# Pooled attention and two feed-forwards: the second one's products in blocks of 384 tokens over two batches, with another table of ranks

## The chip, the cores and the metric

The kernel runs on one core of a Trainium2 chip. Its metric is device time in microseconds, as the median over runs; lower is better. Beside the timed runs there is one execution that the hardware profiler recorded; all rows below are from that one.

## The reference, cut to what matters

The three stages run one after the other on 4 batches, 8 heads, 1152 keys and 576 pooled queries of 64 values, so on 2304 tokens of 512 values. The inputs are float32.

```python
q_pool = q.reshape(B, H, S // 2, 2, D).mean(axis=3)
p = exp(scores - max);  attn = p / (sum(p) + 1e-9);  x = attn @ v       # scores = q_pool k^T / 8
x = (s * relu(x @ w_in) ** 2 + b) @ w_out                               # d_ff 2048
out = (sigmoid(x @ w_gate) * (x @ w_val)) @ w_out2                      # d_ff 1536
```

## The kernel before, in words

All matrix products run on TensorE (PE) in a 32-bit format with fewer bits than float32, so each operand is split into a high part and a low part (`hi`, `lo`), and a product is three matmuls: high by high, high by low, low by high (`mm3`, lines 529 to 535; the three matmuls are lines 531, 532 and 533 for both feed-forwards). The split of a tile is a cast for the high part (line 455 on ScalarE, line 457 on GpSimd) and a subtraction for the low part (line 465, on VectorE or GpSimd). ScalarE is ACT in the rows, VectorE is DVE, GpSimd is POOL.

A batch is 576 tokens (`SQ`), half of one is 288 (`HQ`). The attention of batch 0 is laid out by rows (`pair_rows`), the others by columns (`pair_half`): scores (line 760), a running maximum, its transposition (773) and spreading (738), subtraction (468), exponential (786), split, and the products with the values (808, 809 for the high part, 813 for the low part). The first feed-forward (`ffn1`) runs once per batch, and its matmuls stand between those of the attention of the next batch. The second (`ffn2`) runs twice, each time over two batches: the first call for batches 0 and 1, then the first feed-forward of batch 3, then the second call for batches 2 and 3.

In `ffn2` a feature tile is 128 of the 1536 hidden features. For each one the weights of gate and value are fetched, decoded on three engines (lines 489 to 499) and split into one of four slots called `w` (`ROOM`, w=4), and the gate and value products are made with `up`: per batch and half, 12 matmuls of 288 columns into a PSUM bank for the gate and 12 for the value. Sigmoid (line 1023, ACT), product (line 468, DVE) and a split into `h` follow. After each four feature tiles come the products with `w_out2` (lines 1038 to 1040, 512 columns), 12 for each of nine tiles of 128 tokens. Three `raw` slots hold weights that are being decoded.

The order of all instructions on all engines is planned in Python before the program is written. `Plan.order` walks through time with assumed durations; whenever an engine is free it takes, of the operations whose inputs and slots are at hand, the one with the lowest rank. A rank is a number for the kind of work plus an amount from the table `MOVED` (lines 38 to 151), and ties go by the place in the program plus a second amount from that table. So a change of that table, or of what the operations are, can move any instruction. Each engine then works through its own list in order; what it waits for on the chip are semaphores of the single tiles.

Of the kernel before, what the change touches and what calls it, by code (L numbers as in the profile page):

```python
# [11 lines left out]
F32 = mybir.dt.float32  # L12
F32R = mybir.dt.float32r
AF = mybir.ActivationFunctionType
ALU = mybir.AluOpType
# [23 lines left out]
    "q load": (8, -97),  # L39
    "k load": (16, 21),  # L40
    "v load": (58, -139),
    "v hi": (-33.5, 17),
    "v lo": (-5, -53),
    "q add": (56.5, -16),
    "q twice": (60, -3),
    "pr qT": (0, -105),
    "pr q hi False": (1.5, -26),
    "pr q lo False": (10, 70),
    "pr q hi True": (40, 70),
    "pr q lo True": (4, -76),  # L50
    "pr kT": (-7, 0),
    "pr k hi": (-23.5, 64),
    "pr k lo": (4.5, 94),
    "s b load": (51, 101),
    "r qk 1": (0, 436),
    "r max": (20, 94),
    "r - max": (-33.5, 116),
    "r exp": (59.5, -13),
    "r pT": (-31, -29),
    "r p": (-29.5, -47),  # L60
    "r p hi": (-7.5, -76),
    "r p lo": (-26.5, 53),
    "r pv": (-40, 67),
    "r pT hi": (-20, 30),
    "r pT lo": (32.5, 157),
    "r o": (-40, 104),
    "r x add": (27, -30),
    "r qk 2": (-29, -108),
    "r sums": (1.5, -33),
    "r sums eps": (-0.5, -100),  # L70
    "r 1 / sums": (30, -110),
    "r spread": (-40, -92),
    "r rows": (-3, 63),
    "r rows mid": (0, 533),
    "r x / sums": (0.5, 3),
    "r x / sums mid": (52, 49),
    "r end": (-1, -100),
    "ps qT": (-6.5, -120),
    "ps q hi False": (60, 55),
    "ps q lo False": (-21, 2),  # L80
    "ps kT": (-16, 90),
    "ps k hi": (2, 116),
    "ps k lo": (-33.5, 42),
    "xx hi": (8, 64),
    "xx lo": (0, -25),
    "w load": (-40, -77),
    "w top": (-14.5, 44),
    "w scale": (-24.5, -15),
    "w low": (-21, -21),
    "w join": (0, 65),  # L90
    "w sign": (-30, -67),
    "w hi": (-33, -111),
    "w lo": (-40, 113),
    "w keep": (-34.5, 128),
    "ff xx up": (42.5, -17),
    "ff relu": (0, -85),
    "square": (0.5, 119),
    "g hi": (0.5, 88),
    "g lo": (-2, 74),
    "ff down": (31, 10),  # L100
    "column sums": (60, -1),
    "column sum": (37.5, 56),
    "ff y": (-28.5, 61),
    "ff y add": (19, 52),
    "bias": (0, -21),
    "y bias": (0, -25),
    "y store": (0, -54),
    "qk": (3.5, -109),
    "s copy": (4, -73),
    "s max": (7.5, 39),  # L110
    "max T": (0.5, 25),
    "max": (60, 105),
    "max rows": (26.5, 9),
    "s - max": (22, -81),
    "exp": (0, 89),
    "p hi": (-29.5, 0),
    "p lo": (54.5, -68),
    "pv hi": (22, 11),
    "pv lo": (31, 60),
    "sums": (26, -2),  # L120
    "x": (38, -115),
    "sums out": (-35, 44),
    "sums in": (-9.5, 84),
    "1 / sums spread": (0, -60),
    "1 / sums out": (-12, -13),
    "1 / sums in": (22.5, -70),
    "x / sums": (17, 25),
    "1 / sums": (24.5, -96),
    "w fetch": (-8, 31),
    "w come": (0, -52),  # L130
    "x store": (-3, -88),
    "turn": (-9, -110),
    "yy load": (16.5, -72),
# [4 lines left out]
    "gate val": (-25.5, 123),
    "h hi": (0, -7),
    "h lo": (59.5, 88),  # L140
    "down 2": (-7, 35),
    "out": (-23, -57),
    "out add": (11, -115),
    "out store": (0, -50),
    "xx load": (-40, 35),
    "p2 xx up": (-1.5, 75),
    "p2 relu": (0, -42),
    "p2 down": (0, 97),
    "p2 y": (0, -29),
    "p2 y add": (8, 19),  # L150
# [986 lines left out]
```

## Time and profile before

| what | us |
|---|---|
| median of three runs | 1469.33 (1465.91 to 1474.76) |
| the profiled execution's own time | 1465.83 |
| its span, first to last instruction | 1464.1 |
| PE busy in the span | 1402.4 (96%) |
| DVE, ACT, POOL busy | 1075.5, 944.4, 777.3 |

Matmuls are pipelined: one lasts some 295 ns in the record while the next starts 133 ns after it. So how long a row of matmuls takes is read from the distance of their starts, and "busy" is the time in which at least one runs.

### The profile page before, as it was taken

The numbers are of one execution on the slowest core, as the hardware profiler recorded it, in microseconds if no ns is written. First come the engines' busy times: TensorE is split into PE (matmuls) and PEld (weight loads), VectorE is DVE, ScalarE is ACT, GpSimd is POOL, SyncE is SP. The second block draws the span as 40 slices with busy tenths as digits, with TensorE's granted clock in tenths as the row PEclk, the third lists the DMA queues.
The fourth block names the chain that finished last, engine by engine and source line by source line (L and its number), as shares of the span: only waits on it lengthen the run. The fifth ranks groups of instructions, "written<-read, shape, count | busy, mean of one in ns | idle before, by whom it ended". The sixth has DMA issues, their size and how long they took to land. (4 is left out here: it accounts for less than half of the span.)

```text
span 1464.1 us, 26453 instructions
## 1 busy us (share of the span) xinstructions
PE 1402.4 (96%) x9868; PEld 1334.4 (91%) x9868; DVE 1075.5 (73%) x1775; ACT 944.4 (65%) x2017; POOL 777.3 (53%) x641
## 2 busy tenths in 40 slices
PE   7988999999889999999999999999999999999998
PEld 6877889988889999999899999989898999989897
DVE  6889898799888888889889656848583127847562
ACT  6899888888788989898989734434141534433130
POOL 3677566778766666656747535726151004726130
PEclk9999999999999999999999999999999999999999
DMA  3335132455442324142432374513144444323122
GB/s 90 93 113 194 38 103 91 147 170 164 141 138 103 114 81 137 32 152 72 138 111 75 109 270 148 176 53 122 36 138 126 154 160 144 109 71 109 36 67 65
DMA packets 103049, 167.97 MB, mean 115 GB/s; under 512 B 44652, under 2 KB 80264, under 8 KB 93832
## 3 DMA queue, kind: packets, MB, share of 16 engines
q1 hardware_dynamic: 96008, 115.95, 25.6%
q0 software_dynamic: 6912, 50.33, 9.8%
q8 instruction: 77, 1.26, 0.4%
q14 instruction: 52, 0.43, 0.1%
HBM read 139.99 MB, written 26.28 MB: 114 GB/s over the span
## 5 line engine op out<-in xcount | busy, mean ns | idle before, releaser
L465 POOL TENSOR_TENSOR pp<-st,pp 128x864 fp32r<-128x864 f32 x106 | 226.5, 2144 | 47.5 <-ACT pp L455 41.2
L532 PE MATMUL banks<-yy,w 128*128 128x288 f32 x768 | 226.3, 295 | 0.4 <-DVE yy L465 0.4
L533 PE MATMUL banks<-yy,w 128*128 128x288 f32 x768 | 226.4, 295 | 0.0
L531 PE MATMUL banks<-yy,w 128*128 128x288 f32 x768 | 226.0, 294 | 0.0
L462 ACT COPY st<-banks 128x288 f32<-128x288 f32 x432 | 153.7, 409 | 43.3 <-PE banks L760 35.6
L468 DVE TENSOR_TENSOR mx<-banks,mx 128x288 f32<-128x288 f32 x336 | 151.5, 451 | 22.8 <-ACT st L462 12.9
L760 PE MATMUL banks<-qT,kT 128*128 128x288 f32 x864 | 163.0, 302 | 5.2 <-DVE mx L468 2.6
L531 PE MATMUL banks<-xx,w 128*128 128x288 f32 x512 | 155.6, 304 | 4.6 <-DVE mx L468 2.4
L533 PE MATMUL banks<-xx,w 128*128 128x288 f32 x512 | 151.6, 296 | 0.0
L532 PE MATMUL banks<-xx,w 128*128 128x288 f32 x512 | 151.5, 296 | 0.0
L468 DVE TENSOR_TENSOR st<-st,banks 128x864 f32<-128x864 f32 x144 | 149.3, 1043 | 2.7 <-PE banks L738 2.6
L532 PEld LDWEIGHTS banks<-yy,w 128*128 128x128 f32 x768 | 144.0, 188 | 1.0 <-DVE yy L465 0.6
L531 PEld LDWEIGHTS banks<-yy,w 128*128 128x128 f32 x768 | 144.1, 188 | 0.4
L533 PEld LDWEIGHTS banks<-yy,w 128*128 128x128 f32 x768 | 144.0, 188 | 0.0
L786 ACT ACTIVATE st<-st 128x864 f32<-128x864 f32 x144 | 132.9, 933 | 12.9 <-DVE st L468 12.0
L489 POOL TENSOR_SCALAR raw<-raw 128x512 f32<-128x512 f32 x102 | 84.2, 826 | 106.1 <-DMA raw<-in_moe_w_gate_dram 43.3
L760 PEld LDWEIGHTS banks<-qT,kT 128*128 128x128 f32 x864 | 127.7, 188 | 11.1 <-DVE mx L468 5.6
L531 PE MATMUL banks<-g,w 128*128 128x288 f32 x448 | 135.5, 302 | 0.9 <-DVE mx L468 0.8
L533 PE MATMUL banks<-g,w 128*128 128x288 f32 x448 | 132.0, 295 | 0.0
L532 PE MATMUL banks<-g,w 128*128 128x288 f32 x448 | 132.0, 295 | 0.0
L808 PE MATMUL banks<-pp,vt 128*128 128x288 f32 x432 | 123.6, 306 | 5.3 <-ACT pp L455 2.4
L492 ACT ACTIVATE raw<-raw 128x512 f32<-128x512 f32 x104 | 71.6, 688 | 75.7 <-POOL raw L489 73.6
(150 smaller groups left out, 3968.2 us busy)
## 6 DMA issues: line engine op xcount, KB each, us to landing
w<-d_1u_1u POOLq DMA_DIRECT2D x24, 1024.0 KB, 5.9
w<-d_1d_1d POOLq DMA_DIRECT2D x24, 1024.0 KB, 5.7
raw<-in_moe_w_out_dram SPq DMA_DIRECT2D x40, 512.0 KB, 3.6
raw<-in_moe_w_gate_dram SPq DMA_DIRECT2D x24, 512.0 KB, 4.8
raw<-in_moe_w_val_dram SPq DMA_DIRECT2D x24, 512.0 KB
qn<-in_q_dram SPq DMA_DIRECT2D x16, 576.0 KB, 4.0
kn<-in_k_dram SPq DMA_DIRECT2D x32, 288.0 KB, 4.6
vn<-in_v_dram SPq DMA_DIRECT2D x32, 288.0 KB, 3.2
```

What stands on the lines that cost most here:

```text
L462: act(name, n, lambda: nc.scalar.copy(out=out(), in_=in_()), r, w, rank, sbuf=False)
L465: shared(name, n, lambda e: ENGINE[e].tensor_tensor(out=out(), in0=in0(), in1=in1(), op=op), r, w, rank, 2.15)
L468: dve(name, n, lambda: nc.vector.tensor_tensor(out=out(), in0=in0(), in1=in1(), op=op), r, w, rank)
L489: shared("w top", 512, lambda e: ENGINE[e].tensor_scalar(out=words(1).bitcast(F32), in0=words(1).bitcast(F32), scalar1=F64_TOP, scalar2=-F ...
L492: act("w scale", 512, lambda: nc.scalar.mul(words(1).bitcast(F32), words(1).bitcast(F32), 2.0 ** -112), [], [top], rank)
L531: nc.tensor.matmul(ps(), lhsT=whi(), rhs=xhi(), start=first, stop=False)
L532: nc.tensor.matmul(ps(), lhsT=whi(), rhs=xlo(), start=False, stop=False)
L533: nc.tensor.matmul(ps(), lhsT=wlo(), rhs=xhi(), start=False, stop=last)
L760: nc.tensor.matmul(ps.t[:, :HQ], lhsT=kT.t[:, c], rhs=qq[:, w, hf * HQ:(hf + 1) * HQ], start=(w == 0), stop=(w == 1))
L786: act("exp", 3 * HQ, lambda s=s: nc.scalar.activation(out=s.t, in_=s.t, func=AF.Exp), [], parts, AT)
L808: nc.tensor.matmul(acc.t[:, :HQ], lhsT=vt.t[:, 3 * i + c, D:], rhs=hi.t[:, c], start=(i == c == 0), stop=False)
```

## The change

The gate and value products are made in blocks of `TB` = 384 tokens over the two batches of a call, three blocks in place of four halves of 288. For that the input of a call lies in one tile over both batches (`yy`, one slot of 1152 columns in place of two of 576), `up` takes a slice of tokens instead of a half, and sigmoid, product and split work on 384 columns. The split's parts are now kept apart by block, and a tile of 128 tokens in the second product lies in one block, where before the middle one lay in two batches. Every entry of the table `MOVED` has other numbers.

```diff
-    yy=2, yl=1, h=4, fo=9,
+    yy=1, yl=1, h=4, fo=9,
...
-    "p2 yy up": (57.5, 61),
-    "gate": (-40, 69),
+    "p2 yy up": (51, -50),
+    "gate": (22, 37),
...
+    TB = 384
...
-    def up(tag, xx, w, hf, to):
+    def up(tag, xx, w, cs, to):
         ph = bank(tag)
-        cs = slice(hf * HQ, (hf + 1) * HQ)
+        n = cs.stop - cs.start
+        bs = range(cs.start // SQ, (cs.stop - 1) // SQ + 1)
         for kk in range(KC):
...
-                f"{tag} {xx.tag} up", lambda: ph.t[:, :HQ], HQ,
+                f"{tag} {xx.tag} up", lambda: ph.t[:, :n], n,
...
-                [ph, (w, 0), (w, 1), (xx, 0, kk), (xx, 1, kk)], kk == 0, kk == KC - 1, [to],
+                [ph, (w, 0), (w, 1), *((xx, i, kk, b) for i in range(2) for b in bs)], kk == 0, kk == KC - 1, [to],
...
     def ffn2(b0, nb, gate, here=None):
-        yy = [load_split("fy", "yy", y_d[b0 + b], [("y_d", b0 + b)], gate, here if b == nb - 1 else None) for b in range(nb)]
+        yy = slot("fy", "yy", [P, 2, KC, nb * SQ], F32R)
+        for b in range(nb):
+            load_split("fy", "yy", y_d[b0 + b], [("y_d", b0 + b)], gate, here if b == nb - 1 else None, yy, b)
...
-                for b in range(nb):
+                for i in range(nb * SQ // TB):
                     r = slot("fr", "r", [P, SQ])
-                    bs = slice(b * SQ, (b + 1) * SQ)
-                    for hf in range(2):
-                        cs = slice(hf * HQ, (hf + 1) * HQ)
-                        pg = up("p2", yy[b], wg, hf, r)
-                        pv = up("p2", yy[b], wv, hf, r)
-                        act("gate", HQ, lambda r=r, cs=cs, pg=pg: nc.scalar.activation(
-                            out=r.t[:, cs], in_=pg.t[:, :HQ], func=AF.Sigmoid), [pg], [(r, hf)], FE, sbuf=False)
-                        tt_dve("gate val", HQ, lambda r=r, cs=cs: r.t[:, cs], lambda pv=pv: pv.t[:, :HQ],
-                               lambda r=r, cs=cs: r.t[:, cs], ALU.mult, [pv], [(r, hf)], FE)
-                    split_g(gg, lambda gg=gg, bs=bs: gg.t[:, 0, bs], lambda gg=gg, bs=bs: gg.t[:, 1, bs], r,
-                            (gg, 0, b), (gg, 1, b))
+                    cs = slice(i * TB, (i + 1) * TB)
+                    pg = up("p2", yy, wg, cs, r)
+                    pv = up("p2", yy, wv, cs, r)
+                    act("gate", TB, lambda r=r, pg=pg: nc.scalar.activation(
+                        out=r.t[:, :TB], in_=pg.t[:, :TB], func=AF.Sigmoid), [pg], [r], FE, sbuf=False)
+                    tt_dve("gate val", TB, lambda r=r: r.t[:, :TB], lambda pv=pv: pv.t[:, :TB],
+                           lambda r=r: r.t[:, :TB], ALU.mult, [pv], [r], FE)
+                    split_g(gg, lambda gg=gg, cs=cs: gg.t[:, 0, cs], lambda gg=gg, cs=cs: gg.t[:, 1, cs],
+                            lambda r=r: r.t[:, :TB], TB, [r], (gg, 0, i), (gg, 1, i))
...
-                bs = sorted({m * P // SQ, ((m + 1) * P - 1) // SQ})
+                block = m * P // TB
```

The planned order differs on every engine; two places are shown. Line numbers of the changed kernel are one higher up to `up` and two higher behind it. In the names, `g`, `h` and `xx` are split inputs, a number behind a name is the tile's.

**The first call of `ffn2`.** PE before: the last products of batch 2's first feed-forward (tiles `g_927`, `g_929` with the weights `w_931`) and what follows them.

```order
L532 MATMUL banks_105<-g_927_10824,w_931_10753 128x288
L533 MATMUL banks_105<-g_927_10824,w_931_10753 128x288
L531 MATMUL banks_105<-g_929_10886,w_931_10753 128x288
L532 MATMUL banks_105<-g_929_10886,w_931_10753 128x288
L533 MATMUL banks_105<-g_929_10886,w_931_10753 128x288
L531 MATMUL banks_105<-yy_1149_10502,w_1161_10778 128x288
L532 MATMUL banks_105<-yy_1149_10502,w_1161_10778 128x288
L533 MATMUL banks_105<-yy_1149_10502,w_1161_10778 128x288
L531 MATMUL banks_105<-yy_1151_10629,w_1161_10778 128x288
L532 MATMUL banks_105<-yy_1151_10629,w_1161_10778 128x288
```

They all stand ahead of the second gate product of the call (`yy_1149` and `yy_1151` are the two batches, `w_1161` the first gate and value weights). PE in the changed kernel: the same kind of products (weights `w_930`), behind the first four feature tiles and the nine token tiles of the call, at the point where the fifth feature tile's weights `w_1194` are first used.

```order
L532 MATMUL banks_105<-g_929_10984,w_931_10748 128x288
L533 MATMUL banks_105<-g_929_10984,w_931_10748 128x288
L534 MATMUL banks_105<-g_929_10984,w_931_10748 128x288
L532 MATMUL banks_105<-g_922_10757,w_930_10735 128x288
L533 MATMUL banks_105<-g_922_10757,w_930_10735 128x288
L534 MATMUL banks_105<-g_922_10757,w_930_10735 128x288
L532 MATMUL banks_105<-g_924_10800,w_930_10735 128x288
L533 MATMUL banks_105<-g_924_10800,w_930_10735 128x288
L534 MATMUL banks_105<-g_924_10800,w_930_10735 128x288
L532 MATMUL banks_105<-yy_1148_10505,w_1194_11472 128x384
L533 MATMUL banks_105<-yy_1148_10505,w_1194_11472 128x384
```

So in the changed kernel the two slots `w_930` and `w_931` are held through most of the first call, and the call's own weights pass through the other two. POOL in the changed kernel, around the two instructions that write the value half of `w_1194`, whose slot was that of `w_1188`:

```order
L466 TENSOR_TENSOR h_1184_11233<-r_1186_11225,h_1184_11233 128x384
L458 TENSOR_SCALAR w_1191_11299<-raw_1193_11210 128x512
L466 TENSOR_TENSOR w_1191_11299<-raw_1193_11210,w_1191_11299 128x512
L490 TENSOR_SCALAR raw_1196_11316<-raw_1196_11316 128x512
L490 TENSOR_SCALAR raw_1202_11331<-raw_1202_11331 128x512
L458 TENSOR_SCALAR w_1194_11472<-raw_1196_11316 128x512
L466 TENSOR_TENSOR w_1194_11472<-raw_1196_11316,w_1194_11472 128x512
L490 TENSOR_SCALAR raw_1203_11490<-raw_1203_11490 128x512
L490 TENSOR_SCALAR raw_1209_11506<-raw_1209_11506 128x512
```

Before, this engine writes parts of the tile `w_1191` of the same feature tile; its slot was that of `w_1173`, whose last matmul stands a whole group of products earlier.

```order
L465 TENSOR_TENSOR w_1191_11413<-raw_1192_11281,w_1191_11413 128x512
L465 TENSOR_TENSOR w_1191_11413<-raw_1193_11331,w_1191_11413 128x512
L457 TENSOR_SCALAR h_1182_11477<-r_1183_11391 128x576
L465 TENSOR_TENSOR h_1182_11477<-r_1183_11391,h_1182_11477 128x576
L489 TENSOR_SCALAR raw_1199_11451<-raw_1199_11451 128x512
L489 TENSOR_SCALAR raw_1204_11467<-raw_1204_11467 128x512
L457 TENSOR_SCALAR w_1197_11591<-raw_1199_11451 128x512
L465 TENSOR_TENSOR w_1197_11591<-raw_1199_11451,w_1197_11591 128x512
```

**One softmax of the attention of batch 1.** PE before, at the spreading of its maximum (`mc_493`) and then, 24 matmuls of `xx_275` after it, up to its first product with the values (`pp_494`):

```order
L809 MATMUL banks_105<-pp_485_4054,vt0_121 64x288
L738 MATMUL banks_105<-ident_60,mc_493_4083 128x96 x3
L531 MATMUL banks_105<-xx_275_905,w_324_3578 128x288
L532 MATMUL banks_105<-xx_275_905,w_324_3578 128x288
L533 MATMUL banks_105<-xx_275_905,w_324_3578 128x288
L531 MATMUL banks_105<-xx_275_905,w_324_3578 128x288
```

```order
L760 MATMUL banks_105<-qT_447_3635,kT_449_3586 128x288 x6
L813 MATMUL banks_105<-pp_486_4126,vt0_121 128x288 x3
L808 MATMUL banks_105<-pp_487_4130,vt0_121 128x288
L809 MATMUL banks_105<-pp_487_4130,vt0_121 64x288
L808 MATMUL banks_105<-pp_487_4130,vt0_121 128x288
L809 MATMUL banks_105<-pp_487_4130,vt0_121 64x288
L808 MATMUL banks_105<-pp_487_4130,vt0_121 128x288
L809 MATMUL banks_105<-pp_487_4130,vt0_121 64x288
L760 MATMUL banks_105<-qT_447_3635,kT_449_3586 128x288 x2
L813 MATMUL banks_105<-pp_488_4160,vt0_121 128x288 x3
L760 MATMUL banks_105<-qT_447_3635,kT_449_3586 128x288 x2
L808 MATMUL banks_105<-pp_494_4185,vt1_122 128x288
```

PE in the changed kernel, the same piece, whole:

```order
L775 MATMUL banks_105<-ident_60,mx_492_4021 96x128 x3
L762 MATMUL banks_105<-qT_447_3634,kT_449_3576 128x288 x6
L740 MATMUL banks_105<-ident_60,mc_493_4192 128x96 x3
L762 MATMUL banks_105<-qT_447_3634,kT_449_3576 128x288 x2
L532 MATMUL banks_105<-g_321_3936,w_331_3992 128x288
L533 MATMUL banks_105<-g_321_3936,w_331_3992 128x288
L534 MATMUL banks_105<-g_321_3936,w_331_3992 128x288
L810 MATMUL banks_105<-pp_494_4223,vt1_122 128x288
```

Between the spreading and the first product stood 46 matmuls; now 5 do.

## Rows read from the trace of the kernel before

**Rows 1.** The page's head and part 1: span; busy time and share of each engine

```profile
span 1464.1 us, 26453 instructions
PE 1402.4 (96%) x9868; PEld 1334.4 (91%) x9868; DVE 1075.5 (73%) x1775; ACT 944.4 (65%) x2017; POOL 777.3 (53%) x641
```

**Rows 2.** Busy time by stage: stretch, length, engines, granted clock, DMA share, GB/s

```profile
0.00:172.00 172.00, 146.50 (x972) 132.15 (x973) 143.57 (x318) 145.19 (x415) 107.91 (x127) 0.96 0.36 109
172.00:845.00 673.00, 644.14 (x4750) 616.94 (x4750) 584.25 (x976) 582.22 (x1207) 441.13 (x311) 0.99 0.36 116
845.00:1464.10 619.10, 611.76 (x4150) 585.30 (x4148) 347.64 (x481) 216.95 (x397) 228.23 (x204) 1.00 0.36 115
```

**Rows 3.** PE's waits from 845 us on: releaser, us in total, times, longest

```profile
PE banks L531 <- DMA w<-d_1u_1u: 2.1, 2, 1.5
PE banks L532 <- DVE yy L465: 0.4, 1, 0.4
```

**Rows 4.** Groups of instructions: shapes, count, busy us, mean ns, idle before

```profile
L531 PE MATMUL banks<-yy,w 128*128 128x288 f32 x768 | 226.0, 294 | 0.0
L468 DVE TENSOR_TENSOR r<-banks,r 128x288 f32<-128x288 f32 x96 | 43.4, 452 | 59.3 <-PE banks L533 55.6 <-ACT r L1023 1.7 <-ACT w L455 1.4
L468 DVE TENSOR_TENSOR fo<-banks,fo 128x512 f32<-128x512 f32 x36 | 24.8, 691 | 56.5 <-PE banks L1040 56.3
L465 DVE TENSOR_TENSOR pp<-st,pp 128x864 fp32r<-128x864 f32 x38 | 48.9, 1286 | 5.3 <-ACT pp L455 4.2 <-POOL pp L457 0.8
L465 POOL TENSOR_TENSOR pp<-st,pp 128x864 fp32r<-128x864 f32 x106 | 226.5, 2144 | 47.5 <-ACT pp L455 41.2 <-PE banks L533 2.9 <-DMA raw<-in_moe_w_out_dram 0.8
L468 DVE TENSOR_TENSOR st<-st,banks 128x864 f32<-128x864 f32 x144 | 149.3, 1043 | 2.7 <-PE banks L738 2.6
L786 ACT ACTIVATE st<-st 128x864 f32<-128x864 f32 x144 | 132.9, 933 | 12.9 <-DVE st L468 12.0
L455 ACT CAST pp<-st 128x864 fp32r<-128x864 f32 x110 | 101.2, 921 | 0.7
L455 ACT CAST w<-raw 128x512 fp32r<-128x512 f32 x88 | 58.2, 667 | 67.9 <-DVE raw L499 36.7 <-PE banks L1040 18.0 <-PE banks L533 12.6
L465 DVE TENSOR_TENSOR w<-raw,w 128x512 fp32r<-128x512 f32 x40 | 40.9, 1030 | 18.7 <-ACT w L455 18.7
```

**Rows 5.** PE in order of time, second call, 288 columns: start, us, line, shapes

```profile
1349.85 0.29 PE L533 MATMUL banks<-yy,w 128*128 128x288 f32 x1
...
1352.91 0.29 PE L532 MATMUL banks<-yy,w 128*128 128x288 f32 x1
```

**Rows 6.** PE in order of time, second call, 512 columns

```profile
1283.12 0.39 PE L1039 MATMUL banks<-w,h 128*128 128x512 f32 x1
...
1290.83 0.39 PE L1040 MATMUL banks<-w,h 128*128 128x512 f32 x1
```

**Rows 7.** PE in order of time, scores of batch 0, 384 columns

```profile
27.48 1.98 PE L891 MATMUL banks<-kT,qT 128*128 128x384 f32 x10
27.73 0.51 PE L891 MATMUL banks<-kT,qT 128*128 128x384 f32 x2
28.95 0.51 PE L891 MATMUL banks<-kT,qT 128*128 128x384 f32 x2
```

**Rows 8.** POOL in order of time: a weight slot filled as soon as PE leaves it

```profile
965.44 0.67 POOL L457 TENSOR_SCALAR w<-raw 128x512 fp32r<-128x512 f32 x1 [12.35 <-PE banks L533]
966.20 1.77 POOL L465 TENSOR_TENSOR w<-raw,w 128x512 fp32r<-128x512 f32 x1
```

**Rows 9.** PE, DVE and POOL in order of time, where batch 3 enters the second call

```profile
1240.16 0.29 PE L531 MATMUL banks<-yy,w 128*128 128x288 f32 x1
1240.84 0.40 PE L532 MATMUL banks<-yy,w 128*128 128x288 f32 x1 [0.38 <-DVE yy L465]
1236.77 0.51 DVE L637 SCALAR_TENSOR_TENSOR xy<-banks,s_sb,xy 128x288 f32<-128x288 f32 x1
1238.92 1.87 DVE L465 TENSOR_TENSOR yy<-xy,yy 128x576 fp32r<-128x576 f32 x1
1231.92 0.74 POOL L457 TENSOR_SCALAR yy<-xy 128x576 fp32r<-128x576 f32 x1
1232.75 1.75 POOL L465 TENSOR_TENSOR yy<-xy,yy 128x576 fp32r<-128x576 f32 x1
1232.22 0.29 PE L531 MATMUL banks<-yy,w 128*128 128x288 f32 x1
```

**Rows 10.** PE's longest waits from 172 to 845 us

```profile
PE banks L531 <- DVE mx L468: 3.2, 3, 2.4
PE banks L813 <- POOL pp L465: 3.1, 6, 1.2
```

More of the change, by code (lines that the diff above doesn't have):

```diff
@@ L38 @@
 MOVED = {
[L39 to L133, printed above, removed]
@@ L134 @@
-    "yy hi": (13.5, 59),
-    "yy lo": (0, -93),
-    "p2 yy up": (57.5, 61),
-    "gate": (-40, 69),
[L138 to L150, printed above, removed]
+    "q load": (32, -5),
+    "k load": (33.5, 3),
+    "v load": (45.5, -117),
@@ new lines @@
+    "v hi": (-38, -97),
+    "v lo": (2, -108),
+    "q add": (0, -82),
+    "q twice": (19, 27),
+    "pr qT": (0, 101),
+    "pr q hi False": (5, -93),
+    "pr q lo False": (20, 103),
+    "pr q hi True": (12, 120),
+    "pr q lo True": (-8, -119),
+    "pr kT": (-18.5, -55),
+    "pr k hi": (-5, -44),
+    "pr k lo": (-10, -71),
+    "s b load": (30, -129),
+    "r qk 1": (0, 189),
+    "r max": (33.5, -59),
+    "r - max": (-40, 91),
+    "r exp": (57, -26),
+    "r pT": (-40, 55),
+    "r p": (-4.5, 57),
@@ new lines @@
+    "r p hi": (1, -106),
+    "r p lo": (-40, -100),
+    "r pv": (-40, -109),
+    "r pT hi": (0, 83),
+    "r pT lo": (36.5, 15),
+    "r o": (-40, -167),
+    "r x add": (35.5, -40),
+    "r qk 2": (-17.5, 92),
+    "r sums": (-34, 21),
+    "r sums eps": (3.5, 149),
+    "r 1 / sums": (0, -9),
+    "r spread": (-40, -44),
+    "r rows": (0, -88),
+    "r rows mid": (0, 279),
+    "r x / sums": (-1.5, -118),
+    "r x / sums mid": (52, -15),
+    "r end": (0, 96),
+    "ps qT": (2, -29),
+    "ps q hi False": (60, 90),
@@ new lines @@
+    "ps q lo False": (-37, -29),
+    "ps kT": (-37.5, 16),
+    "ps k hi": (23.5, 77),
+    "ps k lo": (0, 7),
+    "xx hi": (38, -89),
+    "xx lo": (0, 93),
+    "w load": (-1, -143),
+    "w top": (-18.5, 97),
+    "w scale": (-8, 23),
+    "w low": (-19, 3),
+    "w join": (11, 15),
+    "w sign": (-36.5, 3),
+    "w hi": (-40, 67),
+    "w lo": (-40, 124),
+    "w keep": (1, -49),
+    "ff xx up": (59, 10),
+    "ff relu": (-16, -95),
+    "square": (-2.5, -142),
+    "g hi": (7.5, 83),
+    "g lo": (0, -7),
@@ new lines @@
+    "ff down": (52.5, 72),
+    "column sums": (60, 35),
+    "column sum": (30, 111),
+    "ff y": (5, 96),
+    "ff y add": (16.5, -46),
+    "bias": (-10, -34),
+    "y bias": (60, 105),
+    "y store": (-21, -30),
+    "qk": (33, -11),
+    "s copy": (21, 43),
+    "s max": (14, 112),
+    "max T": (29, -81),
+    "max": (60, 64),
+    "max rows": (24.5, -22),
+    "s - max": (16, 71),
+    "exp": (1, 151),
+    "p hi": (-40, 84),
+    "p lo": (6.5, -89),
+    "pv hi": (15, -72),
+    "pv lo": (36, -18),
@@ new lines @@
+    "sums": (31.5, -144),
+    "x": (44, 118),
+    "sums out": (1, -73),
+    "sums in": (3, 38),
+    "1 / sums spread": (6.5, 129),
+    "1 / sums out": (56, 107),
+    "1 / sums in": (22, -4),
+    "x / sums": (0, 61),
+    "1 / sums": (46.5, -68),
+    "w fetch": (-5.5, 3),
+    "w come": (-40, 82),
+    "x store": (28, 26),
+    "yy load": (35.5, -43),
+    "yy hi": (-5.5, -14),
+    "yy lo": (0, 48),
+    "p2 yy up": (51, -50),
+    "gate": (22, 37),
+    "gate val": (-40, 130),
+    "h hi": (-4.5, -101),
@@ L151 @@
+    "h lo": (-36.5, 79),
+    "down 2": (-16, -101),
+    "out": (0.5, 5),
+    "out add": (1.5, -9),
+    "out store": (0, 9),
+    "xx load": (1.5, -33),
+    "p2 xx up": (23, -29),
+    "p2 relu": (8, -42),
+    "p2 down": (33.5, 24),
+    "p2 y": (1.5, 110),
+    "p2 y add": (60, 59),
 }
@@ L535, in mm3, with load_split @@
         pe(name, 3 * mm(n), issue, reads[1:], [reads[0]], FP, to)
-    def load_split(pool, tag, src, key, gate=(), here=None):
+    def load_split(pool, tag, src, key, gate=(), here=None, to=None, b=0):
         xf = here or slot(pool, "xy" if pool == "fx" else "yl", [P, KC, SQ])
@@ L597, in ffn1 @@
                     cs = slice(hf * HQ, (hf + 1) * HQ)
-                    ph = up(fp, xx, w, hf, r)
+                    ph = up(fp, xx, w, cs, r)
                     act(f"{fp} relu", HQ, lambda r=r, cs=cs, ph=ph: nc.scalar.activation(
@@ L1043, in ffn2 @@
                        [*((s, w) for s in w3 for w in range(2)),
-                        *((s, w, b) for s in g for w in range(2) for b in bs)], [po], FP, [o[m]])
+                        *((s, w, block) for s in g for w in range(2))], [po], FP, [o[m]])
                 if f0 == 0:
```

22 lines of the change are left out of this document (11 added, 11 removed).

## The prediction

> **What bounds the kernel now.** I read first the head of the page and its busy shares: in a span of 1464.1 us PE is busy for 1402.4 us, 96%, and the next engine, DVE, for 73% [rows 1]. Next the busy time by stage [rows 2], because such a share is an average. Up to 172 us (batch 0's attention, by rows) PE stands idle for 172.0 − 146.5 = 25.5 us; from there to 845 us (the other attentions between first feed-forwards) for 673.0 − 644.1 = 28.9 us, with DVE and ACT both at 87%; from 845 us to the end (feed-forwards alone) for 7.3 us, and there no other engine is above 56%. Third, PE's waits in the last stage: two on a DMA, 2.1 us together, and one on the low part of `yy`, 0.4 us [rows 3]. So the end is set there by nothing but the row of matmuls: what a matmul's start waits after the one before it, times their number. In the middle stage PE's time counts too, but a late softmax adds to it at once: its longest waits are on the maximum (3.2 us in three) and on `pp` low (3.1 us in six) [rows 10]. The granted clock is 0.96, 0.99 and 1.00 in the three stages [rows 2], the upper level throughout, and the change leaves PE no idler, so I give the clock no term.
>
> **Part 1, the products' shape.** Each of the three matmuls of gate and value occurs 768 times with 288 columns [rows 4], so 2304 in all. The columns stay the same, 2304 × 288 = 663,552, and blocks of 384 make 1728 matmuls of them, 576 fewer. The price is the distance of starts. With 288 columns: (1352.91 − 1349.85) / 23 steps = 0.1330 us [rows 5]. With 512 columns: (1290.83 − 1283.12) / 34 = 0.2268 us [rows 6]. A line through both gives 0.1330 + 96 × 0.000419 = 0.1732 us for 384. The kernel before has matmuls of 384 columns too, in batch 0's scores: seven steps from 27.73 to 28.95 give 0.1743 us, and ten in 1.98 us with the record of the last (0.34 taken off) 0.182 us, an upper bound since one in that row waited [rows 7]. Before: 2304 × 0.1330 = 306.4 us. After: 1728 × 0.1732 = 299.3 (−7.1), × 0.1743 = 301.2 (−5.2), × 0.182 = 314.5 (+8.1). I take the middle of the first two, −6.2 us, because both are rows of matmuls that waited for nothing. All of it lies on the path, since these products stand in the stage where PE doesn't wait.
>
> The saving is the fixed part of a step: by the line above, 0.1330 − 288 × 0.000419 = 0.012 us, which 576 steps fewer save. The Trainium skill (TensorE: Matmul & The Clock Gate, section Back-to-back issue gap) gives columns / 2.4 GHz plus 2.5 ns for one matmul by itself; by that formula, as an estimate, 576 × 2.5 ns = 1.4 us would be saved, while its sustained 131 ns for 512 columns would make PE's whole stage shorter than it is. The trace's 0.2268 us at 512 columns agrees with neither, and it decides; the small saving is the third rival below.
>
> **Part 2, what stands beside those products.** ACT's sigmoid, DVE's product and the split go from 96 pieces to 72 each. DVE's product costs 452 ns with 288 columns and 691 with 512 [rows 4], so 0.554 us with 384: 43.4 us become 39.9. In the last stage DVE has 619 − 348 = 271 us free and ACT 402 [rows 2], under PE's matmuls: 0 on the path. If that cover were gone the end would still move by no more than those few us, and downward. One `yy` tile in place of two means that the second call's load can begin only when the first call has read all of it; a whole first feed-forward of batch 3 lies between, so 0.
>
> Where batch 3 enters the second call, PE waited 0.54 us for `yy`: the matmul due at 1240.16 + 0.133 started at 1240.84 [rows 9]. DVE's last sum ends at 1236.77 + 0.51 = 1237.28, and its low part, 1238.92 to 1240.79, was what PE had waited for. Counted from the first `yy` matmul at 1232.22, the part of batch 3 came due after 61 matmuls of 288, 8.1 us; in the changed order it comes due after 43 of 384, 7.5 us, and its split is on POOL, 0.74 + 1.75 us [rows 9] behind the sum, so ready at 5.1 + 2.5 = 7.6 us or somewhat later. A wait of 0.1 to 0.5 us as before: 0.
>
> **Part 3, the weights' slots in the first call.** The new order leaves the 96 last products of batch 2's first feed-forward (weights `w_930` and `w_931`) standing through the call, where before all of them stood ahead of the second gate product. Two of the four slots are held by them, and the call's weights go through the other two. By the planned order seven refills (among them `w_1160`, `w_1167`, `w_1194`) have between the last matmul of the slot's old weights and the first of the new only 2.6 to 4.6 us of PE's work: for `w_1160` 24 matmuls of 288, 24 × 0.133 = 3.2 us; for `w_1194` 6 of 512 and 15 of 288, 1.4 + 2.0 = 3.4 us. Before, such refills had 23 us. What a refill takes when it starts at once is on POOL 965.44 + 0.67, a gap and 1.77, to 967.97: 2.5 us [rows 8]; with the cast on ACT (667 ns) and the low part on DVE (1030 ns) 1.7 us [rows 4] and a hand-over. What queues behind a late one on PE is everything. The gate half is needed first, the value half 12 matmuls of 384 later (2.1 us), so the two need not be ready together. So the wait is between 0 and, if each refill begins only after all the cover has run out (its engines are busy with `h` or a decoding when PE leaves the slot), 7 × (0.67 + 1.77) = 17.1 us. Below nothing it can't be: PE doesn't wait for `w` there now but for the 2.1 us of [rows 3]. I take 0, since 2.5 is under 2.6 and the engines are half free; both ends stay for the range.
>
> **Part 4, the table elsewhere.** In the middle stage almost all stands as before. One softmax of batch 1 doesn't: between the spreading of `mc_493` and the first product of `pp_494` stood 46 matmuls (6.1 us), now 5 (0.67 us). What must happen in between is DVE's subtraction, 1043 ns, ACT's exponential, 933, and the cast of the high part, 921 [rows 4]: 2.9 us, and with hand-overs up to 3.5. PE waits 2.2 to 2.8 us: I take +2.8. Nothing follows it on PE that could run meanwhile, as the queue is in order. For the other 47 units of work the covers add up to somewhat less (207 us between the spreading and the product, from 224; 104 between transposition and spreading, from 117) or more (207 from 201 before the low part's product); I give that 0, and bound it above by two more waits of 2.8 us (the fourth rival) and below by the first rival's gain. Twelve of the `pp` low parts go from POOL (2144 ns, 106 now) to DVE (1286 ns, 38 now) [rows 4]: 15.4 us more on a DVE with 673 − 584 = 89 us free, and earlier by 0.86 us each where PE waits on POOL for them [rows 10]. 0.
>
> **The sum.** −6.2 + 2.8 = −3.4 us. The profiled execution's own time is 1465.83 us, so it would become 1462.4; the median of the runs is 3.5 us above that execution, and the forecast is made for the median: 1469.33 − 3.4 = 1465.9 us.
>
> **The rivals.**
> *The table gives back idle time.* PE's 25.5 + 28.9 = 54.4 idle us before 845 us [rows 2] are what a new order can win. For it: the waits there are many and small [rows 10], so an order can fit better without its gaps showing it. Against: the order there is hardly changed, and where it is, one cover got shorter. A sixth of it, 9 us: 1465.9 − 9.1 = 1456.8.
> *The two slots are late (the slower side).* PE waits at the first use of each of those seven weights in the first call. For it: covers of 2.6 to 4.6 us against the 2.5 us of a refill that starts at once. Against: POOL is busy for 228 of 619 us there [rows 2], and the planner saw this order through with durations of its own. The full price is 17.1 us: 1465.9 + 17.1 = 1483.0. From 0.5 us in each of the seven the change no longer gains; from (7.4 + 3.4) / 7 = 1.5 us it is slower by over 0.5%.
> *Wider blocks save nothing.* If a step of 384 takes 384/288 of one of 288, 0.1773 us, part 1 is 0 and only +2.8 is left: 1472.1. For it the upper figure of [rows 7]; against it the 0.2268 of [rows 6], which is under 0.1330 × 512/288 = 0.2364.
> *Other softmaxes are short as well.* The 17 and 13 us of cover lost are spread thin; if two more units wait 2.8 us each, 1465.9 + 5.6 = 1471.5.
>
> **How the numbers follow.** Chances: forecast 0.45, table gives back 0.20, slots late 0.10, no saving 0.13, softmaxes short 0.12. A measurement of this kernel tells 0.5%, 7.35 us, from no change: faster means under 1462.0, slower over 1476.7. The forecast's own range is 1460 to 1471 (part 1 between −5.2 and −7.1, each hidden term a few us off), and about 0.12 of its 0.45 lies under 1462; of the first rival nearly all, 0.18, and 0.02 of the others: faster 0.32. Slower: most of the slots' 0.10, 0.08, and 0.02 each of the others' upper ends (0.182 us at 384 gives 1469.3 + 8.1 + 2.8 = 1480.2): 0.14. Within: 0.54. The range of 1455 to 1479 leaves out half of the slots' case, the far end of the first rival and of the spacing.
>
> **What would show it.** The three matmul lines of gate and value with 576 pieces each and starts 0.173 to 0.174 us apart (part 1; 0.177 or more is the third rival). In the first call, PE's waits on `w` from POOL, DVE or ACT: under 2 us for part 3, over 4 for the second rival. At `pp_494` one wait of 2 to 3 us (part 4). The stage from 845 us on shorter by about 6 us if it does the same work, and the two stages before it as long as now, within 3 us; if they are shorter by 8 or more, the table won it. I am wrong if the last stage's gain and the first two stages' loss don't come out of these places.

## The result, and the profile after

The changed kernel takes 1456.62 us as the median of 11 runs (1449.44 to 1461.99), the kernel before on the same chip 1471.2 us (11 runs, 1462.16 to 1475.42): a ratio of 0.9913, interval 0.9896 to 0.9931. Two later sets of runs gave 0.9900 [0.9877, 0.9923] and 0.9926 [0.9900, 0.9952]. So the change gains 11 to 15 us; the forecast was a gain of 3.4.

The head of the page after, to be held against [rows 1]:

```profile
span 1460.2 us, 25288 instructions
PE 1395.9 (96%) x9292; PEld 1332.2 (91%) x9292; DVE 1076.8 (74%) x1775; ACT 944.8 (65%) x2008; POOL 763.7 (52%) x650
```

Busy time by stage after, against [rows 2] (stretch, length, then busy time of PE, PEld, DVE, ACT and POOL with their instructions, PE's granted clock, the DMA engines' share and GB/s):

```profile
0.00:172.00 172.00, 146.98 (x974) 132.75 (x975) 143.77 (x320) 145.04 (x415) 107.99 (x127) 0.96 0.36 109
172.00:845.00 673.00, 644.05 (x4784) 621.70 (x4783) 591.62 (x983) 579.06 (x1199) 437.82 (x317) 0.99 0.36 117
845.00:1460.20 615.20, 604.91 (x3539) 577.77 (x3537) 341.40 (x473) 220.66 (x397) 217.88 (x207) 0.99 0.35 115
```

Read by itself, this trace misleads. Its span is only 3.9 us below that of before, because the profiled execution, 1461.99 us, was the longest of the 11 runs, while that of before, 1465.83 us, was shorter than all but one of its 11. Two more traces of the changed kernel have spans of 1452.6 and 1452.8 us, another of the kernel before 1467.3 us. The busy columns don't tell the difference either: up to 845 us PE is as busy as before, since it does more work in the same time.

So I add up what is lost between matmuls. For each two neighbours on PE, the distance of their starts less 0.4167 ns a column and 13.3 ns (133.3 ns for 288 columns and 226.6 for 512, where the unbroken rows of [rows 5, 6] have 133.0 and 226.8) is lost time, be it a wait, a slower clock or a change of shape. Only differences between traces are read from it. Summed over three stretches that are bounded by work, not by time (up to the first score by columns; from there to the last product with the values; the rest), in us:

| table, blocks | traces | rows of batch 0 | attention by columns | rest |
|---|---|---|---|---|
| old, 288 (before) | 2 | 65.6, 66.0 | 88.2, 91.8 | 0.6, −0.2 |
| old, 384 (e1) | 1 | 67.1 | 88.7 | 7.0 |
| new, 288 (e2) | 1 | 62.0 | 81.0 | 12.3 |
| new, 384 (after, e3, e11) | 3 | 65.7, 64.7, 62.1 | 83.6, 81.2, 82.6 | 9.0, 4.8, 6.3 |

With blocks of 384 there are also 576 × 13.3 ns = 7.6 us fewer fixed parts. The means of before and after: 1.6 us less in the rows, 7.5 less in the attention, 7.6 fewer fixed parts, and 6.5 more in the rest (2.5 of them in the products' own row, whose step is a little over that line, 2.2 in longer waits, 1.4 at a lower clock behind these), together 10.2; the mean spans, 1465.7 and 1455.2 us, differ by 10.5.

The products' row in order of time (start, duration, line, shapes), nine matmuls of one row in the second call:

```profile
1349.70 0.33 PE L532 MATMUL banks<-yy,w 128*128 128x384 f32 x1
...
1351.09 0.33 PE L534 MATMUL banks<-yy,w 128*128 128x384 f32 x1
```

(1351.09 − 1349.70) / 8 = 0.174 us, the value of [rows 7], and not the 0.182. The sum of all distances from a gate or value product to the next matmul is 305.9 us before and 300.8 after: 5.1 us saved, 9 ns for each matmul fewer.

PE's waits from 845 us on, which answer to [rows 3]:

```profile
PE banks L532 <- DMA w<-d_1u_1u: 5.0, 2, 2.7
PE banks L534 <- POOL w L466: 0.3, 1, 0.3
```

Two groups of DVE, which answer to [rows 4]:

```profile
L469 DVE TENSOR_TENSOR r<-banks,r 128x384 f32<-128x384 f32 x72 | 39.8, 553 | 48.3 <-PE banks L534 46.2 <-ACT r L1025 1.9
L466 DVE TENSOR_TENSOR pp<-st,pp 128x864 fp32r<-128x864 f32 x50 | 66.3, 1327 | 13.2 <-ACT pp L456 12.2 <-POOL pp L458 0.9
```

The weights that pass through two slots cost 0.3 us, so the seven refills come in time. What grew is another wait, for weights of the first feed-forward that are kept in DRAM and fetched back (`d_1u_1u`, the kept weights): 2.1 and 1.2 us in the two traces of before, 5.0 here, 3.4 and 3.6 in the other two traces of the changed kernel. For the `pp` low parts on DVE, now 50, PE waits 1.1 us in all. And the one softmax of batch 1, PE in order of time, with the idle time ahead of a row and its releaser in brackets:

```profile
342.26 0.29 PE L534 MATMUL banks<-g,w 128*128 128x288 f32 x1
346.47 0.61 PE L810 MATMUL banks<-pp,vt 128*128 128x288 f32 x1 [3.92 <-ACT pp L456]
```

The same place by stretches; the granted clock is the third number from the right:

```profile
342.00:347.00 5.00, 1.08 (x7) 0.83 (x6) 5.00 (x9) 4.12 (x7) 4.76 (x5) 0.86 0.52 167
347.00:349.00 2.00, 2.00 (x11) 1.92 (x10) 0.44 (x2) 2.00 (x4) 2.00 (x2) 0.50 0.90 202
349.00:351.00 2.00, 2.00 (x11) 1.99 (x11) 0.85 (x2) 1.65 (x3) 2.00 (x2) 0.50 1.06 438
351.00:353.00 2.00, 2.00 (x12) 2.00 (x12) 1.40 (x3) 1.59 (x5) 2.00 (x3) 0.63 0.31 131
353.00:355.00 2.00, 2.00 (x17) 2.00 (x16) 2.00 (x5) 2.00 (x5) 1.39 (x1) 1.00 0.00 0
```

PE waits 3.9 us there, where 2.2 to 2.8 were forecast, and then runs at 1.2 GHz for over 5 us: 11 matmuls in 2 us in place of 17.

### The profile page after: what moved, and what is told of

Read it like the earlier page. It is cut to its first block, busy times and chain, and to the rows that moved or that the text cites. A ratio compares the mean times of both kernels' runs of the same rounds, so it can differ in the third digit from the quotient of the medians.

```text
span 1460.2 us, 25288 instructions
## 1 busy us (share of the span) xinstructions
PE 1395.9 (96%) x9292; PEld 1332.2 (91%) x9292; DVE 1076.8 (74%) x1775; ACT 944.8 (65%) x2008; POOL 763.7 (52%) x650
## 5 line engine op out<-in xcount | busy, mean ns | idle before, releaser
L466 POOL TENSOR_TENSOR pp<-st,pp 128x864 fp32r<-128x864 f32 x94 | 202.5, 2161 | 33.8 <-ACT pp L456 27.8
L534 PE MATMUL banks<-yy,w 128*128 128x384 f32 x576 | 192.6, 334 | 0.3 <-POOL w L466 0.3
L533 PE MATMUL banks<-yy,w 128*128 128x384 f32 x576 | 192.6, 334 | 0.1
L532 PE MATMUL banks<-yy,w 128*128 128x384 f32 x576 | 192.5, 334 | 0.0
L469 DVE TENSOR_TENSOR mx<-banks,mx 128x288 f32<-128x288 f32 x336 | 150.6, 449 | 15.6 <-ACT st L463 8.1
L490 POOL TENSOR_SCALAR raw<-raw 128x512 f32<-128x512 f32 x99 | 78.4, 792 | 129.1 <-DMA raw<-in_moe_w_gate_dram 40.9
L810 PE MATMUL banks<-pp,vt 128*128 128x288 f32 x432 | 122.3, 303 | 10.6 <-ACT pp L456 7.9
L811 PE MATMUL banks<-pp,vt 128*64 128x288 f32 x432 | 119.5, 296 | 0.0
L466 POOL TENSOR_TENSOR w<-raw,w 128x512 fp32r<-128x512 f32 x64 | 100.3, 1569 | 19.8 <-ACT w L456 18.6
L494 DVE TENSOR_SCALAR raw<-raw 128x512 uint32<-128x512 uint32 x104 | 74.1, 715 | 47.2 <-DMA raw<-in_moe_w_val_dram 18.3
```

Of the source, the lines that this page charges most:

```text
L466: shared(name, n, lambda e: ENGINE[e].tensor_tensor(out=out(), in0=in0(), in1=in1(), op=op), r, w, rank, 2.15)
L469: dve(name, n, lambda: nc.vector.tensor_tensor(out=out(), in0=in0(), in1=in1(), op=op), r, w, rank)
L490: shared("w top", 512, lambda e: ENGINE[e].tensor_scalar(out=words(1).bitcast(F32), in0=words(1).bitcast(F32), scalar1=F64_TOP, scalar2=-F ...
L494: dve("w low", 512, lambda: nc.vector.tensor_scalar(out=words(0), in0=words(0), scalar1=29, scalar2=None, op0=ALU.logical_shift_right,), [ ...
L532: nc.tensor.matmul(ps(), lhsT=whi(), rhs=xhi(), start=first, stop=False)
L533: nc.tensor.matmul(ps(), lhsT=whi(), rhs=xlo(), start=False, stop=False)
```

## The experiments

The theories by their letters: A, the two parts add up, 5 us from the blocks and the rest from the table; B, the blocks give all; C, a table fits only the code that it was chosen for. D and E are on the wait for kept weights: POOL's order, or the transfers themselves. F and G: the wait at the softmax has a price of its own, or DVE is full there. H and I: a part of the table carries the gain, or it is one piece. Each run below is timed against the kernel before on its own chip.

**The two halves of the change (e1, e2).** e1 is the changed kernel with the table of before; e2 the kernel before with the new table.

```diff
 MOVED = {
-    "q load": (32, -5),
+    "q load": (8, -97),
...
```

> The blocks of 384 with the old table of ranks. Theory A (the two parts add up, the blocks give the 5 us by which the traces' rows of gate and value products differ, 305.9 to 300.8 us, and the table the rest): ratio to before about 0.9965, some 1466 us, and a last stage (from the last product with the values on) shorter by about 5 us with the stages before it as long as before. Theory B (the blocks give the whole difference): 0.991, some 1458 us. Theory C (a table fits only the code that it was chosen for; a foreign one makes new waits in the attention): slower than before, 1.002 or more, with more idle time of PE before 845 us than the 54.4 us of before, though the row of products is 5 us shorter.

> Blocks of 288 as before with the new table of ranks. Theory A: ratio to before about 0.994, some 1463 us, the gain in the stages before 845 us. Theory B: 1.000, 1471 us. Theory C: slower than before, 1.002 or more, by waits in the attention; the products' row as long as before, 306 us.

Measured: e1 1470.45 us, 1.0016 [0.9994, 1.0038]; e2 1470.65 us, 1.0001 [0.9984, 1.0018]. Neither half gains anything by itself, and both together gain 14 us. By the times that is Theory C. The traces say otherwise. In e2 the attention lost 81.0 us, less than any trace with the old table, and in e1 the row of products was 302.6 us against 305.9. The gains are there, and each is lost again in the last stage: 7.0 and 12.3 us in the table above, against about 0 before. In e1 the 3.3 us that the row gains meet 5.2 us of waits there, in place of 2.5 and 1.7; this is read from its trace alone, no run moves anything in it. PE's longest waits from 842 us on in e1:

```profile
PE banks L533 <- DMA w<-d_1u_1u: 3.8, 3, 1.9
PE banks L534 <- POOL yy L467: 0.6, 1, 0.6
PE banks L1043 <- POOL h L467: 0.5, 1, 0.5
```

And in e2, from 845 us on:

```profile
PE banks L530 <- DMA w<-d_1u_1u: 8.5, 2, 6.3
PE banks L530 <- DMA w<-d_1d_1d: 1.0, 1, 1.0
PE banks L532 <- DVE w L464: 0.3, 1, 0.3
```

**The same kernels again (e3, e4).** No edit.

> The changed kernel once more, for a second trace. Its first trace was of one of the longest of its executions (1462.0 us, median 1456.6). If what varies between executions are waits for transfers (5.0 us at two waits for the first feed-forward's weights in that trace, 2.1 before), a shorter execution shows under 3 us there and as much as 3 us less in all; if it is the many short waits of the attention, the stage up to 845 us differs. Ratio 0.990 to 0.993.

> The kernel before once more, for a second trace and for what no change looks like: ratio 0.998 to 1.002. Its first trace was of one of its shorter executions (1465.8 us, median 1471.2). A longer one shows either longer waits for transfers (over 4 us at the two waits for weights) or more idle time before 845 us than 54.4 us.

Measured: e3 1455.17 us, 0.9900 [0.9877, 0.9923]; e4 1469.15 us, 0.9988 [0.9966, 1.0010]. Both accounts of the spread hold in part. In e3's trace the waits for kept weights are 3.4 us, not the under 3 that was expected, but PE kept its clock behind them:

```profile
PE banks L532 <- DMA w<-d_1u_1u: 3.4, 2, 1.7
```

The first trace of the changed kernel by stretches, at the first of those waits and behind it:

```profile
859.00:862.00 3.00, 0.26 (x2) 0.24 (x2) 0.76 (x1) 2.01 (x5) 1.91 (x2) 0.84 1.00 366
862.00:864.00 2.00, 2.00 (x9) 2.00 (x10) 0.00 (x0) 0.00 (x0) 0.00 (x0) 0.50 1.02 406
864.00:866.00 2.00, 2.00 (x10) 2.00 (x9) 0.00 (x0) 0.89 (x3) 1.50 (x3) 0.50 0.82 311
```

The same place in e3:

```profile
855.00:858.00 3.00, 1.26 (x10) 1.06 (x9) 0.41 (x1) 2.46 (x5) 1.91 (x2) 1.00 1.00 385
858.00:860.00 2.00, 2.00 (x17) 2.00 (x16) 0.34 (x1) 0.41 (x1) 0.00 (x0) 1.00 1.00 402
```

One microsecond more of waiting (2.7 us against 1.7) was followed by half clock until almost 868 us, which cost 2.8 us more. e4's longer span lies in the attention, 91.8 us lost against 88.2, with 1.2 us of waits for weights: there the expectation of over 4 us was wrong, the other one right.

**The fetches ahead of the splits (e5, e6).** Where does e2's wait of 6.3 us come from? POOL in e2 in order of time; ahead of it PE's last product with the weights whose slots the next fetches take:

```profile
1121.02 0.39 PE L1039 MATMUL banks<-w,h 128*128 128x512 f32 x1
...
1123.57 1.32 POOL L456 TENSOR_SCALAR yy<-yl 128x576 fp32r<-128x576 f32 x2 [13.64 <-DMA yl<-y_d]
1124.85 3.85 POOL L464 TENSOR_TENSOR yy<-yl,yy 128x576 fp32r<-128x576 f32 x2
1128.64 1.15 POOL L512 DMA_DIRECT2D w<-d_1d_1d  x2
1129.77 0.55 POOL L512 DMA_DIRECT2D w<-d_1u_1u  x1
...
1140.42 0.58 PE L530 MATMUL banks<-xx,w 128*128 128x288 f32 x1 [6.30 <-DMA w<-d_1u_1u]
```

The slots are free from 1121.4 us on, but the fetches stand on POOL behind four pieces of batch 2's `yy`, which wait for their load and aren't needed before 1233 us. So two transfers of 1 MB start 7 us late, and the third, which PE needs first, lands 10.6 us after its issue behind them. In e5 (from e2) and e6 (from the changed kernel) these pieces are moved behind the fetches on POOL, and in the first call one piece behind one fetch; PE's order stays the same to the row.

```diff
+        for i in reversed([i for i in pool if self.names[i] in ("yy hi", "yy lo")]):
...
+            far = [x for x in pool[at + 1:at + (2 if first else 8)] if self.names[x] == "w fetch"]
...
+                    out.insert(b, out.pop(a))
...
-        for i in self.order():
+        for i in self.hoisted(self.order()):
```

> Blocks of 288 with the new table, and on GpSimd the fetches of the kept weights (1 MB each, for the first feed-forward of batch 3, and one for batch 2's) stand ahead of the splits of yy, which wait for their load; PE's order is the same to the row. In e2 the stage up to the last value product had 8 us less lost between matmuls than before, and PE then waited 6.3 us at 1134 us for such a weight and ran at half clock until 1146. Theory D (the table's gain is real and was lost at that one place, since the fetch stood behind the split): the wait falls under 1.5 us, and the ratio to before is 0.994 to 0.996 (some 1462 us; e2 1470.7). Theory E (the transfers themselves are late, at 400 GB/s beside the output's): the wait falls by less than 1.5 us and the ratio stays at 0.999 to 1.001.

> The changed kernel with the same edit. Its two waits for kept weights were 5.0 us in one trace and 3.4 in the other. Theory D: under 2 us together, and 1452 us, a ratio of 0.987 to 0.989. Theory E: as now, 3 to 5 us, 0.990 to 0.991.

Measured: e5 1461.56 us, 0.9943 [0.9921, 0.9965], 9 us below e2 (8.5 by the ratios; the chips differ); e6 1452.56 us, 0.9897 [0.9874, 0.9921]. POOL and PE in e5:

```profile
1121.25 0.57 POOL L535 DMA_DIRECT2D w<-d_1d_1d  x1 [10.42 <-PE banks L1062]
1122.61 0.53 POOL L535 DMA_DIRECT2D w<-d_1d_1d  x1 [0.79 <-PE banks L1062]
1128.96 0.53 POOL L535 DMA_DIRECT2D w<-d_1u_1u  x1 [5.82 <-PE banks L555]
...
1136.45 0.37 PE L553 MATMUL banks<-xx,w 128*128 128x288 f32 x1 [1.42 <-DMA w<-d_1u_1u]
```

The wait falls from 6.3 to 1.4 us, the stretch at half clock behind it is gone, and the rest loses 0.9 us in place of 12.3; the attention still loses 81.9. That is Theory D: the table is worth 8 us by itself, and e2 lost it at that one queue. The edit wasn't run on the kernel before, where those waits are 2.1 and 1.2 us in all. In e6 the two waits come to 2.3 us, slightly above the expected under 2, and its ratio lies between the ranges of D and E, with an interval that covers both.

**Blocks of 288 in the changed code (e7).**

```diff
-    TB = 384
+    TB = 288
...
-                block = m * P // TB
+                blocks = sorted({m * P // TB, ((m + 1) * P - 1) // TB})
```

> The changed kernel (one yy tile, new table) with four blocks of 288 in place of three of 384; PE's order up to the first product of the second feed-forward is the same. Theory A/D (the blocks are worth the fixed part of 576 matmuls, 5 us in the traces): 1455.2 + 5 = 1460 us, ratio 0.993 to 0.995, the row of products 306 us. Theory C (the table fits only the blocks that it was chosen for): new waits in the last stage, 1465 us or more, 0.997 or more.

Measured: 1465.67 us, 0.9984 [0.9966, 1.0001], some 10 us more than with 384, as Theory C had it (0.997 or more). Six of them are the row of products, 306.9 us against 300.8, and one of these six is the two waits of 0.6 us below, which stand in it. The last stage lost 9.4 us, with 4.4 us of waits for kept weights and four of 0.5 or 0.6:

```profile
PE banks L532 <- DMA w<-d_1u_1u: 4.4, 2, 2.2
PE banks L534 <- POOL w L466: 0.6, 1, 0.6
PE banks L533 <- DVE yy L466: 0.6, 1, 0.6
PE banks L1042 <- POOL h L466: 0.5, 1, 0.5
PE banks L1040 <- ACT h L456: 0.5, 1, 0.5
```

So both theories hold for about half each: 5 us are the matmuls', and some 5 the order's, which the planner makes anew when the pieces change.

**The softmax that PE waits for, put first (e8).** Its first third's subtraction, exponential and cast go ahead of a maximum on DVE and of copies and a weight's cast on ACT.

```diff
+        i = [x for x in out if self.names[x] == "max rows"][unit]
+        for name in ("s - max", "exp", "p hi"):
...
+            out.insert(a, out.pop(b))
```

> The changed kernel; of the one softmax that PE waits 3.9 us for (pp_494, at 342 us) the first third's subtraction, exponential and cast stand ahead of a maximum and a weight's operations on DVE and of copies and a weight's cast on ACT. Theory F (that wait and the stretch at half clock behind it, 347 to 352.5 us, are a price of their own): the wait falls to some 2.5 us, and the ratio is 0.987 to 0.989. Theory G (DVE is busy without a gap from 338 to 347 us, so what is put first there makes the next unit's maximum late by as much): the wait moves to the next transposition, ratio 0.990 to 0.991.

Measured: 1459.3 us, 0.9940 [0.9917, 0.9963]: by the ratios 2 to 6 us worse than the changed kernel, with intervals that overlap. PE's waits there, in order of time:

```profile
344.03 0.61 PE L827 MATMUL banks<-pp,vt 128*128 128x288 f32 x1 [2.68 <-ACT pp L473]
346.70 0.88 PE L792 MATMUL banks<-ident,mx 128*96 128x128 f32 x3 [0.86 <-DVE mx L486]
355.19 0.66 PE L832 MATMUL banks<-pp,vt 128*128 128x288 f32 x3 [0.90 <-POOL pp L483]
```

The wait fell to 2.7 us as wanted, and came back at the next unit's maximum and at its low part; over the attention 88.6 us were lost in place of 81 to 84. Theory F is out, and the wait moved as Theory G has it. Only 1.5 to 2 us of the difference arise at this place. Most of the remainder, 1.4 to 5 us, arises between 380 and 400 us, where PE waits 2.0 us for a maximum; the changed kernel's first trace has the same wait and its other two don't, so no run shows that the edit caused it.

**The table in two parts (e9, e10).** The kernel before, with the new numbers for the 28 kinds of work of the attention by columns alone (e9), and for the other 84 alone (e10).

```diff
-    "qk": (3.5, -109),
+    "qk": (33, -11),
...
```

> The kernel before with the new table's numbers for 28 kinds of work alone, those of the attention by columns (scores, maxima, softmax, products with the values, sums, transposed q and k); the other 84 as before. Theory H (the gain in the attention comes from the order of its own operations): time lost between PE's matmuls from the first column score to the last value product 81 to 84 us, as with the whole new table (88 to 92 before), ratio 0.994 to 0.997. Theory I (a table is one piece; half of a new one meets the old other half at other moments): 90 us or more lost there, ratio 1.001 or more.

> The kernel before with the new numbers for the other 84 kinds (batch 0's rows, weights, both feed-forwards) and the old ones for the 28 of the attention by columns. Theory H: 88 to 92 us lost in the attention, ratio 0.999 to 1.003. Theory I: 90 us or more, ratio 1.001 or more. If instead this half gives the gain (81 to 84 us lost), it lies in when the feed-forward's matmuls and the weights' decoding come between the attention's.

Measured: e9 1552.97 us, 1.0573 [1.0542, 1.0604]; e10 1492.79 us, 1.0164 [1.0133, 1.0195]. Lost in the attention: 150.6 and 106.3 us. PE's longest waits in e9:

```profile
PE banks L531 <- ACT w L455: 20.9, 1, 20.9
PE banks L760 <- DVE mx L468: 9.5, 15, 0.8
```

And in e10:

```profile
PE banks L808 <- ACT pp L455: 15.5, 6, 6.8
PE banks L531 <- DMA w<-d_1u_1u: 9.1, 2, 7.1
```

Theory I: the numbers mean something only relative to each other. Which of them carry the 8 us can't be told in this way.

**The changed kernel beside e6's (e11, e12).**

> The changed kernel once more, to stand on one chip beside the next run: ratio 0.990 to 0.992.

> The changed kernel with the fetches of kept weights ahead of the splits of yy, once more. If its gain is the 1 to 3 us of shorter waits for those weights seen in its trace (2.3 us against 5.0 and 3.4): a ratio lower by 0.001 to 0.002 than that of the changed kernel beside it. If the 3 us between their medians were the chips' difference: the same ratio within 0.001.

Measured on one chip: e11 1458.84 us, 0.9926 [0.9900, 0.9952]; e12 1455.5 us, 0.9906 [0.9879, 0.9932]. The 3 us of the first comparison are there again, and the expected 0.002 of the ratio, but the intervals overlap. e12's waits for kept weights are 2.3 us, e11's 3.6. So the kernels with the fetches ahead have the lowest medians, by about 3 us, which these runs don't settle.

## Why the prediction came out as it did

**The number.** The measured 1456.6 us lies inside the stated range (1455 to 1479), 1.6 us from its fast end, and 9 us under the forecast. The range held it; the sum did not. The prediction's own sign for the table, the first two stages shorter by 8 us or more, came out: 1.6 + 7.5 = 9.1 us less lost there.

**Part 1, the blocks: right.** The step is 0.174 us and the row saves 5.1 us; forecast −6.2, between −5.2 and −7.1, so at its small end. "Wider blocks save nothing" is out. The 2.5 ns that the Trainium skill (TensorE: Matmul & The Clock Gate, section Back-to-back issue gap) gives for one matmul by itself would, as an estimate, have saved 1.4 us; the runs here don't agree.

**Part 2: right where it can be seen.** DVE's product took 553 ns (0.554 forecast), and nothing of these pieces shows among PE's waits but 0.3 us in some traces.

**Part 3, the two slots: right.** PE's waits for weights that POOL fills came to 0.3 us in all. The second rival is out: a refill takes less than its cover even where that is 2.6 us.

**Part 4, the one softmax: the place was right, its size not.** The wait was 3.9 us, not 2.8: the chain of three operations was counted without what stands between them on DVE and ACT, a weight's sign and a maximum, and copies and a weight's cast. And the half clock behind it was not counted, 1.7 to 3.1 us more in the three traces. The prediction gave the clock no term, since it read the means of 0.96 and 0.99 [rows 2] as the upper level throughout. They are not: the kernel before itself falls below it for short stretches, as behind the wait of 2.4 us of [rows 10] (PE alone: stretch, length, busy time, granted clock, DMA share, GB/s):

```profile
410.00:412.00 2.00, 1.52 (x6) 0.55 0.09 33
412.00:414.00 2.00, 2.00 (x12) 0.60 0.00 0
```

Over the attention such stretches lose as much with either table (4.3 and 8.3 us in the two traces of before, 5.6 to 6.6 in the three of the changed kernel), so the table's gain isn't the clock's.

**The failing step: "For the other 47 units of work ... I give that 0".** The attention as a whole loses 7.5 us less with the new table (82.5 in the mean against 90.0), although its one visible wait costs more than forecast. The rival "the table gives back idle time" (9 us, chance 0.20) was what happened, on top of the forecast. That its figure fits is luck: the 9 us were a sixth of PE's idle time, which did not shrink, and 4 us were given back in the last stage. Why I missed it: I had added up the covers between two kinds of steps, which came out slightly smaller. But PE's waits of the middle stage come to 25 to 28 us with either table.

What shrank is too short for the view of waits: it lists idle time of over 0.15 us, and the record of a matmul of 288 columns ends some 0.16 us after the next start is due, so a start up to 0.3 us late leaves no wait. At the full clock and without a listed wait, starts over 0.16 us late are 35 to 39 in the attention of the three traces with the old table (8.8 to 9.9 us) and 20 to 23 in e2 and the three of the changed kernel (4.2 to 5.0 us); all distances at the full clock without a listed wait together lose 7 us less. By the kind of matmul that starts late, before and e4 against the three traces of the changed kernel, the first feed-forward's first products 7.0 and 6.7 us against 0.3 to 2.2; the transposition of the maximum 12.4 and 12.6 against 8.8 to 10.0; the transposition of q and k 13.3 and 13.4 against 10.4. The spreading of the maximum lost more, 8.5 to 11.5 against 7.1 and 7.3. Part of the first products' loss is the wait for `mx` of [rows 10], 3.2 us before and 0.3 to 1.7 after. Which entries of the table do it stays open (e9, e10).

**What the prediction didn't have:** the kept weights. It read [rows 3] as two waits of 2.1 us that stay. With the new order POOL issues these fetches behind a split that waits for a load, and the waits grew to 3.4 to 5.0 us; with the fetches ahead (e6, e12) they are 2.3. I had followed POOL's queue for the second feed-forward's weights only.

**The claim on the last stage** (shorter by about 6 us if it does the same work) failed with that: 5.1 us saved, about 4 given back in waits and in the half clock behind them. And the forecast leaned on one profiled execution. Against a spread of some 12 us between executions the single trace could show the 5 us of a stage, but not the whole.

## What to carry to other kernels

A reordering that moves PE's own order little can still be worth more than the arithmetic it comes with; compare time lost between starts over a whole stage, not the covers of single waits, nor the waits that a view lists. Two parts of a change that each measure nothing can both be real, when each gives its gain back at another place: look in the trace for that place before calling them one piece. An in-order queue that issues fetches should not hold, ahead of them, work that waits for another load and isn't needed for long.

## What the runs showed of the hardware

A wait of PE can cost more than itself. After e2's wait of 6.3 us PE's granted clock was 0.50, which is 1.2 GHz, until about 1146 us: 10 matmuls in 2 us where the rows of e3 above have 17 at the full one. PE by stretches in e2:

```profile
1134.00:1140.00 6.00, 0.13 (x1) 0.00 (x0) 0.76 (x1) 1.76 (x3) 0.53 (x1) 0.68 1.07 419
1140.00:1142.00 2.00, 1.57 (x6) 1.60 (x7) 0.00 (x0) 0.00 (x0) 0.00 (x0) 0.50 1.03 414
1142.00:1144.00 2.00, 2.00 (x10) 2.00 (x10) 0.00 (x0) 0.32 (x1) 0.00 (x0) 0.50 0.02 4
1144.00:1146.00 2.00, 2.00 (x10) 2.00 (x10) 0.00 (x0) 0.09 (x1) 0.00 (x0) 0.50 0.00 0
1146.00:1148.00 2.00, 2.00 (x16) 2.00 (x15) 0.00 (x0) 1.38 (x3) 0.00 (x0) 0.91 0.00 0
```

In the last stage and at the softmax of 342 us, waits of 2.7 us and more were followed by such a stretch in each trace looked at, and of five of 2.0 to 2.3 us three were. The length alone doesn't tell: at one place of the attention, near 371 us, a wait of 1.5 us was followed by one in e4 and e1 and by none in the first trace of before. Such a stretch cost 1.3 to 3.1 us, beside the wait. A small change in a transfer can so become several microseconds in the time: of the 7.6 us between the first two traces of the changed kernel, 4.2 lie in the last stage, and 2.8 of these are one such stretch.
